# Units 1 and 3 to 11: state products and scores issued as one block, in other PSUM banks, with a step's second product moved behind them

## The chip, the cores and the metric

The kernel runs on one core of one Trainium2 chip. Its time is device microseconds from one launch; the figure compared is the median of the runs. TensorE does the matrix products (PE in the profile, PEld for its weight loads), VectorE (DVE), ScalarE (ACT) and GpSimd (POOL) do elementwise work, and SyncE (SP) issues most transfers.

## The reference

Two blocks follow each other. The first is a gated linear attention over 4 batches, 8 heads, 768 tokens and head size 48; the second is a feed-forward layer with ELU from 384 to 2048 and back to 384, on the 3072 tokens of the first:

```python
f = 1.0 / (1.0 + np.exp(-f_logit))
for t in range(S):
    state = f[:, :, t, :, None] * state + np.einsum('bhd,bhe->bhde', k[:, :, t], v[:, :, t])
    y[:, :, t] = np.einsum('bhd,bhde->bhe', q[:, :, t], state)
x = y.transpose(0, 2, 1, 3).reshape(B * S, H * D)
h = x @ w_in
g = np.where(h > 0.0, h, np.exp(np.minimum(h, 0.0)) - 1.0)
out = g @ w_out
```

The two weights arrive in 64-bit floating point and are narrowed on the chip.

## The kernel before

The tokens are cut into 12 units of 256 (three per batch). A unit's attention works in four chunks of 64 tokens; its feed-forward works in 8 positions P, each for 256 of the 2048 inner features.

The whole program is laid out by hand on a time line of steps T, 16 to a unit, two to a position. At an even T the list `plan[T]` runs and then `up(P)` issues the first product of position P; at an odd T `joined(P)` runs first (VectorE's three additions that finish the first product, then ScalarE's exponential), then `plan[T]`, then `down(P - 2)` issues the second product of the position two back. From unit 1 on both products are in a Strassen-like form with seven part products; `up7` writes two PSUM banks of tag `h` (`pa` and `pb`), and the next `up7` writes the same two, so it waits for the first addition `h[:, 0:2]` (for `pa`) and for `joined` (for `pb`). `elu` inside `up7` finishes the activation of the position before and lets GpSimd form `sums` for `down`. `down` accumulates a unit in banks `m0` to `m3`; at the last position ScalarE copies one half bank and VectorE's five additions at L991 read all four banks, before the store.

While unit u-1 runs its feed-forward, `attention(u)` is placed on the same steps. With t = 16(u-1), before the change: transposes of k at t+2 (banks `a0`, `a1`, copied by ScalarE), `advance` at t+4 (the chunks' products of k and v, L728, 64 records of 64x64 products into `a0`, `a1`), `step` for the four chunks at t+5 (VectorE adds each to the running state, L686, L691), `scores` at t+7 (products of q and k, L705, 64 records, also in `a0` and `a1`) followed by `mask` (two VectorE products with the causal mask, L713), `outputs` at t+9 (L743) and `carried` at t+11 (L763). Gates of the next unit (`decays`: a scan and a reciprocal on VectorE) stand at t+9, t+11, t+13. The range check of the weights rereads them in 32 pieces: `reread(n)` issues a transfer on SP at step 48+4n and `check(n)` reduces it on VectorE (two instructions, L603) four steps later.

Unit 0 to the first steps of unit 1 are the start: weights are fetched, narrowed on VectorE and ScalarE (L563, L567, L573, L581) and used in the same steps, with a feed-forward of unit 0 in plain form (L927 and L959, banks `m1` and `m2`) while unit 1's attention runs. `warm` issues matrix products that are used by nothing.

Of the kernel before, what the change touches and what calls it, by code (L numbers as in the profile page):

```python
# [356 lines left out]
def fast(ctx: ExitStack, tc: tile.TileContext, q, k, v, f_logit, w_in, w_out, out, flag, outer):  # L357
# [18 lines left out]
    nc = tc.nc  # L376
# [7 lines left out]
    NC = U // C  # L384
    UPB = S // U
    NU = B * UPB
    HP = H // 2
    NFT = DFF // 128
# [5 lines left out]
    LAG = 2  # L394
    AHEAD = 7
    WA = 1
    F1 = (1, 3)
    W0 = 3
    HOLD = 2
    A1 = (2, 5, 6, 8, 10, 11)  # L400
    D2 = (16, 18, 20, 22)
    A2 = (23, 25, 25, 26, 27, 28)
    D3 = (-7, -5, -3, -1)
    A3 = (2, 4, 5, 7, 9, 11)
    BL = 13
    RR = 0
    MX = 10
    CB = 16
    BL1 = 13
# [51 lines left out]
    start = ctx.enter_context(ExitStack())  # L461
# [215 lines left out]
    def step(u, c):  # L677

        if u % UPB == UPB - 1 and c == NC - 1:
            return  # L680
        new = pus[u][c % 2][:, c // 2]
        box = boxes[(u * NC + c) % len(boxes)]
        s = box[:].rearrange("n (p d) -> n p d", d=64)[:, 0:HP, PAD:]
        if u % UPB or c:
            old = sts[u, c][:].rearrange("n (p d) -> n p d", d=64)[:, 0:HP, PAD:]
            nc.vector.tensor_tensor(out=s, in0=new, in1=old, op=ALU.add)  # L686
        else:
            nc.scalar.copy(s, new)
        if c == NC - 1:
            end = qkf[u % NB]["f"][:, :, 1, U - 1 :].broadcast_to([128, HP, D])  # L690
            nc.vector.tensor_tensor(out=s, in0=s, in1=end, op=ALU.mult)  # L691
        sts[(u, c + 1) if c < NC - 1 else (u + 1, 0)] = box
# [25 lines left out]
    def advance(u, pairs=range(HP)):  # L718

        if u not in pus:  # L720
            pus[u] = [ps.tile([128, NW, HP, D], FP32, tag=n, name=f"psU{u}_{n}") for n in ("a0", "a1")]
        pu = pus[u]
        for p in pairs:
            for w in range(NW):
                for r in range(2):
                    h = 2 * p + r
                    for b in range(2):
                        nc.tensor.matmul(  # L728
                            pu[b][FULL[r], w, p], lhsT=kns[u, p // 2][FULL[b], p % 2, w, FULL[r]],
                            rhs=vs[u % NB][FULL[b], w, PAD + h * D : PAD + (h + 1) * D],  # L730
                            start=(w == 0 and p == 0), stop=(w == NW - 1 and p == HP - 1), skip_group_check=True,
                        )
# [91 lines left out]
    def at_step(step, *todo):  # L824
        plan.setdefault(step, []).extend(todo)

    def attention(u, first, then):

        kept = []
        for p, i in enumerate(first):  # L830
            at_step(i, (lambda: settle(u)) if p == NKT else lambda p=p: decays(u, p))
        if u > 1:
            at_step(then[0], lambda: transposed(u, 0, "a0"), lambda: transposed(u, 1, "a1"))
        at_step(then[1], lambda: advance(u))
        at_step(then[2], *(lambda c=c: step(u, c) for c in range(NC)))
        at_step(then[3], lambda: kept.append(scores(u)), lambda: mask(u, kept[0]))
        at_step(then[4], lambda: outputs(u))
        at_step(then[5], lambda: carried(u))

    gs, ss, pms, phs = {}, {}, {}, {}  # L840

# [108 lines left out]
    def down(P):  # L950
        m, j = order[P]
        if j == 0:
            pms[m] = [ps.tile([128, DM], FP32, tag=f"m{i + (m < DIRECT)}", name=f"psM{m}_{i}") for i in range(NW if m < DIRECT else 4)]
        pm, g = pms[m], gs.pop(P)
        ends = dict(start=(j == 0), stop=(j == NP - 1))
        if m < DIRECT:
            for i in range(2):
                for t in range(NW):
                    nc.tensor.matmul(  # L959
                        pm[t][:], lhsT=g[:, i, t * 128 : (t + 1) * 128], rhs=wo[:, 2 * j + i, :],  # L960
                        start=(j == 0 and i == 0), stop=(j == NP - 1 and i == 1),
                    )
            if j == NP - 1:
                o = (outer if (NU - m) % 2 else sb).tile([128, 2, DM], FP32, tag="o", name=f"o{m}", bufs=1)
                for t in range(NW):
                    nc.scalar.copy(o[:, t], pm[t][:])
                    t0 = m * U + t * 128
                    nc.sync.dma_start(out=out[t0 : t0 + 128, :], in_=o[:, t])
                del pms[m]
            return  # L970
        s = ss.pop(P)
        a = [[g[:, i, t * 128 : (t + 1) * 128] for i in range(2)] for t in range(2)]
        b = [[wo[:, 2 * j + i, h * DH : (h + 1) * DH] for h in range(2)] for i in range(2)]
        c = [combos[i][:, j] for i in range(4)]

        for bank, half, x, y in (
            (0, 0, a[0][0], b[0][0]), (3, 0, a[0][1], b[1][0]), (0, 1, s[:, 1], c[1]),
            (1, 0, s[:, 0], c[0]), (1, 1, s[:, 2], c[2]), (2, 1, a[1][1], c[3]), (2, 0, s[:, 3], b[1][1]),
        ):
            first = j == 0 and (bank, half) in ((0, 0), (3, 0), (1, 0), (2, 1))  # L980
            nc.tensor.matmul(  # L981
                pm[bank][:, half * DH : (half + 1) * DH], lhsT=x, rhs=y,
                start=first, stop=(j == NP - 1), skip_group_check=True,
            )
        if j == NP - 1:
            p = [[pm[i][:, h * DH : (h + 1) * DH] for h in range(2)] for i in range(4)]
            o = (outer if (NU - m) % 2 else sb).tile([128, 2, DM], FP32, tag="o", name=f"o{m}", bufs=1)
            u2 = sb.tile([128, DH], FP32, tag="u2", name=f"u2_{m}", bufs=1)
            u43 = sb.tile([128, 2, DH], FP32, tag="u43", name=f"u43_{m}", bufs=1)
            flat = o[:].rearrange("p t f -> p (t f)")  # L990
            add = lambda to, x, y: nc.vector.tensor_tensor(out=to, in0=x, in1=y, op=ALU.add)  # L991
            (nc.vector.tensor_copy if m == NU - 1 else nc.scalar.copy)(u2[:], p[0][0])
            add(flat[:, 0:DH], p[3][0], u2[:])
            add(u2[:], p[0][1], u2[:])
            add(u43[:], pm[1][:].rearrange("p (h f) -> p h f", h=2), u2[:].unsqueeze(1).broadcast_to([128, 2, DH]))
            add(flat[:, 3 * DH :], p[1][0], u43[:, 1])
            add(flat[:, DH : 3 * DH], pm[2][:], u43[:].rearrange("p h f -> p (h f)"))
            def store(*queues):
                for t in range(2):
                    for h in ((1, 0) if t else (0, 1)):  # L1000
                        queues[t].dma_start(
                            out=out[m * U + t * 128 : m * U + (t + 1) * 128, h * DH : (h + 1) * DH],
                            in_=o[:, t, h * DH : (h + 1) * DH],
                        )

            if m == NU - 1:
                left.append(store)
            else:
                store(nc.sync, nc.sync)
            del pms[m]  # L1010
# [18 lines left out]
        nc.tensor.matmul(pf[0:1, :], lhsT=low[:], rhs=causal[:, W - 1 : W], start=True, stop=True)  # L1029
        nc.vector.tensor_copy(flag[:], pf[0:1, :])  # L1030

    def warm(n, bank="m0"):

        pw = ps.tile([128, 4, 128], FP32, tag=bank, name="psW")
        for _ in range(n):
            nc.tensor.matmul(
                pw[:], lhsT=ident[:], rhs=ident[:].unsqueeze(1).broadcast_to([128, 4, 128]), start=True, stop=True
            )
# [81 lines left out]
    at_step(F1[1], lambda: move(1, 1, nc.scalar), lambda: watch(1))  # L1120
    at_step(F1[1] + 2, lambda: scale(1, ("q", NKT, nc.gpsimd)))
    at_step(A1[0], lambda: transposed(1, 0, "a0"), lambda: transposed(1, 1, "a1"))
    attention(1, (), A1)
    at_step(8, lambda: load(2))
    at_step(14, lambda: gates(2))
# [8 lines left out]
    for u in range(3, NU):  # L1134
        t = (u - 1) * NFT
        at_step(t + BL, lambda u=u: blend(u))
        at_step(t - 16, lambda u=u: load(u))
        at_step(t - 8, lambda u=u: gates(u))
        attention(u, [t + i for i in D3], [t + i for i in A3])
    for n in range(NR):  # L1140
        t = 3 * NFT + (NU - 4) * NFT * n // NR + RR
        at_step(t, lambda n=n: reread(n))
        at_step(t + 4, lambda n=n: check(n))
    at_step((NU - 1) * NFT + 9, lambda: finish_flag(0))
    at_step((NU - 1) * NFT + 13, lambda: finish_flag(1))
    for T in range(NU * NFT):
        P = T // 2
        sevens = order[P][0] >= DIRECT
        if T % 2 and sevens:
            joined(P)  # L1150
        if T % 2 == 0 and P and order[P - 1][0] < DIRECT:
            elu(P - 1)
        for f in plan.pop(T, ()):
            f()
        if T % 2 == 0:
            up(P)
        elif P >= LAG:
            down(P - LAG)
        for n in later.pop(T, ()):
            split(n)  # L1160
            lower(n)
# [53 lines left out]
```

## Time and profile before

| | |
|---|---|
| median of 3 runs | 567.14 us (567.03 to 568.18) |
| the profiled execution, first to last instruction | 567.3 us |
| TensorE busy, and its weight loads | 547.5 us (97%), 509.7 us (90%) |
| VectorE, ScalarE, GpSimd busy | 409.4 us (72%), 230.2 us (41%), 292.7 us (52%) |
| first products of the feed-forward in the final chain (L882) | 36% |
| second products in the final chain (L981) | 36% |
| scores, outputs, carried, state products in the final chain | 2% each |
| mean granted TensorE clock | 0.997 |

The page gives the profiled execution's span and no second time for it; the span lies 0.16 us over the median of the runs. The profile's line numbers are those of the kernel listing. An f32 product is recorded as two instructions, so a `down` of seven products is 14 records and an `up7` of ten is 20. In a timeline the first column is the start in us, the second the length of the merged group; groups of a pipelined engine overlap, so the distance from start to start is what a group costs.

### The profile page before, as it was taken

What the parts mean: (1) busy time and instruction counts of PE and PEld (TensorE: products, weight loads), DVE (VectorE), ACT (ScalarE), POOL (GpSimd) and SP (SyncE); (2) the same over time, 40 slices, a digit from 0 to 9 for tenths busy, and PEclk for the clock granted to TensorE, in tenths of its full rate; (3) what the DMA queues carried; (4) which work ended last, traced back from release to release, by engine and by line L of the source; (5) the groups of instructions that cost most, each with busy time, mean ns of one, the idle gap of its engine ahead of it and who ended that gap; (6) DMA issues with size and microseconds to landing.
All of it is one profiled execution on the core that took longest, in us unless ns stands there. A gap on an engine that the chain in (4) does not pass through costs nothing.

```text
span 567.3 us, 15527 instructions
## 1 busy us (share of the span) xinstructions
PE 547.5 (97%) x6336; PEld 509.7 (90%) x6336; DVE 409.4 (72%) x802; ACT 230.2 (41%) x424; POOL 292.7 (52%) x567
## 2 busy tenths in 40 slices
PE   6879998999999999999999999999999999999996
PEld 3566677999999999999999999999999999999996
DVE  8779989785675785885785885786776876745543
ACT  3287862443343433434343343333343343233331
POOL 6601788475374465456366357257248348325332
PEclk9899999999999999999999999999999999999999
DMA  8997951024024225215216216206206203201001
GB/s 212 266 261 209 298 129 43 3 47 114 3 46 138 65 52 145 79 42 156 78 36 155 86 38 153 86 19 173 84 14 178 84 6 74 84 2 36 29 2 35
DMA packets 38193, 53.30 MB, mean 94 GB/s; under 512 B 3712, under 2 KB 27936, under 8 KB 38112
## 3 DMA queue, kind: packets, MB, share of 16 engines
q1 hardware_dynamic: 37312, 51.62, 34.2%
q8 instruction: 52, 0.85, 0.7%
q10 hardware_dynamic: 800, 0.59, 0.4%
q14 instruction: 29, 0.24, 0.1%
HBM read 44.04 MB, written 4.72 MB: 86 GB/s over the span
## 4 chain that ended last, share of the span: by engine, by line
PE 81%; DMA 7%; DVE 7%; issue 2%; POOL 1%; ACT 1%; SPq 0%; DVEq 0%; ACTq 0%; POOLq 0%
PE psH L882 36%; PE psM L981 36%; DMA area<-in_moe_w_in_dram 4%; PE psS L705 2%; PE psY L743 2%; PE psY L763 2%; PE psU_a L728 2%; DVE f L631 2%; PE psT L669 1%; DMA xt<-xt 1%; DMA f<-f 1%; DVE f L626 1%; DMA k<-in_k_dram 1%; DVE bits L563 1%; DVE area L850 1%
## 5 line engine op out<-in xcount | busy, mean ns | idle before, releaser
L882 PE MATMUL psH<-xt,wi 128*128 128x128 f32 (+1 forms) x1056 | 195.0, 294 | 0.1
L946 POOL TENSOR_TENSOR sums<-gg 128x128 f32<-128x128 f32 x176 | 77.7, 462 | 214.5 <-DVE gg L936 205.9
L882 PEld LDWEIGHTS psH<-xt,wi 128*128 128x128 f32 x1056 | 149.5, 192 | 1.8 <-DVE hh L891 0.4
L914 ACT ACTIVATE gg<-hh 128x512 f32<-128x512 f32 x88 | 55.5, 631 | 232.0 <-DVE hh L904 154.6
L882 PE MATMUL psH<-xt,area 128*128 128x128 f32 x704 | 121.8, 275 | 1.3 <-DVE hh L904 1.0
L882 PEld LDWEIGHTS psH<-xt,area 128*128 128x128 f32 x704 | 106.5, 191 | 6.3 <-PE psH L882 1.3
L891 DVE TENSOR_TENSOR hh<-psH,u 128x256 f32<-128x256 f32 x88 | 37.1, 422 | 93.9 <-ACT u L889 93.9
L981 PE MATMUL psM<-area,sums 128*128 128x192 f32 x528 | 100.2, 326 | 0.0
L981 PEld LDWEIGHTS psM<-area,sums 128*128 128x128 f32 x528 | 88.2, 190 | 0.0
L981 PE MATMUL psM<-wo,gg 128*128 128x192 f32 x352 | 74.9, 335 | 0.0
L631 DVE RECIPROCAL f<-f 128x256 f32<-128x256 f32 x36 | 62.7, 1747 | 1.1
L936 DVE SCALAR_TENSOR_TENSOR gg<-gg,hh 128x512 f32<-128x512 f32 x88 | 61.9, 703 | 1.5 <-ACT gg L915 1.5
L915 ACT ACTIVATE gg<-gg 128x512 f32<-128x512 f32 x96 | 60.6, 631 | 3.0
L981 PEld LDWEIGHTS psM<-wo,gg 128*128 128x128 f32 x352 | 55.2, 190 | 2.0
L904 DVE TENSOR_TENSOR hh<-psH,u43h 128x256 f32<-128x256 f32 (+1 forms) x176 | 54.7, 352 | 3.0
L946 POOL TENSOR_TENSOR sums<-gg,sums 128x128 f32<-128x128 f32 x88 | 47.0, 534 | 6.9
L889 ACT COPY u<-psH 128x128 f32<-128x128 f32 x88 | 23.1, 263 | 60.9 <-PE psH L882 60.9
L621 POOL TENSOR_TENSOR q<-q,f 128x256 f32<-128x256 f32 x48 | 35.7, 745 | 21.8 <-DVE f L631 10.6
L904 DVE TENSOR_TENSOR u43h<-psH,hh 128x256 f32<-128x256 f32 x88 | 37.1, 422 | 12.7 <-PE psH L882 12.4
L621 POOL TENSOR_TENSOR k<-k,f 128x256 f32<-128x256 f32 x48 | 40.7, 851 | 7.1 <-DMA f<-f 5.1
L981 PE MATMUL psM<-area,gg 128*128 128x192 f32 x176 | 43.0, 326 | 0.0
L981 PE MATMUL psM<-wo,sums 128*128 128x192 f32 x176 | 43.0, 326 | 0.0
(97 smaller groups left out, 672.3 us busy)
## 6 DMA issues: line engine op xcount, KB each, us to landing
area<-in_moe_w_out_dram SPq DMA_DIRECT2D x8, 768.0 KB, 9.6
again<-in_moe_w_in_dram SPq DMA_DIRECT2D x16, 384.0 KB, 4.2
again<-in_moe_w_out_dram SPq DMA_DIRECT2D x16, 384.0 KB, 3.5
k<-in_k_dram SPq DMA_DIRECT2D x12, 384.0 KB, 4.5
q<-in_q_dram SPq DMA_DIRECT2D x12, 384.0 KB, 5.4
v<-in_v_dram SPq DMA_DIRECT2D x12, 384.0 KB, 5.8
area<-in_moe_w_in_dram SPq DMA_DIRECT2D x8, 576.0 KB, 8.4
out_dram<-o SPq DMA_DIRECT2D x42, 96.0 KB, 1.7
```

Of the source, the lines that this page charges most:

```text
L621: e.tensor_tensor(out=t[n][:, p], in0=t[n][:, p], in1=t["f"][:, p, "kq".index(n)], op=ALU.mult)
L631: nc.vector.reciprocal(f[:, p, 1], f[:, p, 0])
L705: nc.tensor.matmul(pc[r][FULL[b], w, p], lhsT=t["k"][FULL[r], p, cols], rhs=t["q"][FULL[r], p, cols], start=True, stop=True,)
L882: nc.tensor.matmul(to, lhsT=lhs, rhs=rhs, start=(n == 0), stop=True, skip_group_check=True)
L889: nc.scalar.copy(u1[:], pa[:, 0])
L891: add = lambda to, x, y: nc.vector.tensor_tensor(out=to, in0=x, in1=y, op=ALU.add)
L904: add = lambda to, x, y: nc.vector.tensor_tensor(out=to, in0=x, in1=y, op=ALU.add)
L914: nc.scalar.activation(g[:], h, AF.Relu, scale=-1.0)
L915: nc.scalar.activation(g[:], g[:], AF.Exp, scale=-1.0)
L936: nc.vector.scalar_tensor_tensor(out=g[:], in0=g[:], scalar=-1.0, in1=phs.pop(P), op0=ALU.add, op1=ALU.max)
L946: nc.gpsimd.tensor_tensor(out=s[:, i], in0=x, in1=y, op=op)
L981: nc.tensor.matmul(pm[bank][:, half * DH : (half + 1) * DH], lhsT=x, rhs=y, start=first, stop=(j == NP - 1), skip_group_check=True,)
```

## The change

For the ten units 1 and 3 to 11 the list of steps has four entries in place of six. A new function `both` issues at one step `advance`, `scores` into banks `m3` and `m0`, the two masks, and then the four state sums. For units 3 to 11 it stands at t+5, where before the state sums stood; for unit 1 at step 8, where its scores stood. So that `m3` and `m0` are free, the second product of the unit before at that step (its first, j = 0) is left out there and issued two steps later, directly ahead of the next one; its seven products are in another order (the ones for banks 1 and 2 first) at j = 0 of every unit from 1 on. Unit 2 keeps its six steps. All rereads and checks move by two steps (`RR`). At step 4 sixteen products of one element each are added on TensorE, ahead of that step's `up`.

```diff
+    SMALL = 16
+    RR = 2
-    A1 = (2, 5, 6, 8, 10, 11)
+    A1 = (2, 8, 10, 11)
-    A3 = (2, 4, 5, 7, 9, 11)
+    A3 = (2, 5, 9, 11)
-    RR = 0
...
+    def both(u):
+
+        advance(u)
+        mask(u, scores(u, ("m3", "m0")))
+        for c in range(NC):
+            step(u, c)
+
...
-        at_step(then[1], lambda: advance(u))
-        at_step(then[2], *(lambda c=c: step(u, c) for c in range(NC)))
-        at_step(then[3], lambda: kept.append(scores(u)), lambda: mask(u, kept[0]))
-        at_step(then[4], lambda: outputs(u))
-        at_step(then[5], lambda: carried(u))
+        if len(then) == 4:
+            at_step(then[1], lambda: both(u))
+        else:
+            at_step(then[1], lambda: advance(u))
+            at_step(then[2], *(lambda c=c: step(u, c) for c in range(NC)))
+            at_step(then[3], lambda: kept.append(scores(u)), lambda: mask(u, kept[0]))
+        at_step(then[-2], lambda: outputs(u))
+        at_step(then[-1], lambda: carried(u))
...
-        for bank, half, x, y in (
+        todo = [
             (0, 0, a[0][0], b[0][0]), (3, 0, a[0][1], b[1][0]), (0, 1, s[:, 1], c[1]),
             (1, 0, s[:, 0], c[0]), (1, 1, s[:, 2], c[2]), (2, 1, a[1][1], c[3]), (2, 0, s[:, 3], b[1][1]),
-        ):
+        ]
+        if j == 0:
+            todo = todo[3:] + todo[:3]
+        for bank, half, x, y in todo:
...
-    def warm(n, bank="m0"):
+    def warm(n, bank="m0", small=0):
...
+        for _ in range(small):
+            nc.tensor.matmul(pw[0:1, 0, 0:1], lhsT=ident[:, 0:1], rhs=ident[:, 0:1], start=True, stop=True)
...
+    at_step(4, lambda: warm(0, "m3", SMALL))
...
+    joint = [(u - 1) * NFT + A3[1] for u in range(3, NU)]
...
-        elif P >= LAG:
+        elif P >= LAG and T not in joint:
+            if T - 2 in joint:
+                down(P - LAG - 1)
             down(P - LAG)
```

## The prediction

> **What bounds the kernel now.** I read the page's busy shares and chain first, then all waits from 104 us to the end, then TensorE's timeline over one unit, then VectorE's over the same steps.
>
> ```profile
> PE 547.5 (97%) x6336; PEld 509.7 (90%) x6336; DVE 409.4 (72%) x802; ACT 230.2 (41%) x424; POOL 292.7 (52%) x567
> ...
> PEclk9899999999999999999999999999999999999999
> ...
> PE 81%; DMA 7%; DVE 7%; issue 2%; POOL 1%; ACT 1%; SPq 0%; DVEq 0%; ACTq 0%; POOLq 0%
> ```
>
> TensorE is the bound, at full clock; the chain's DMA and DVE shares lie in the first 100 us. Of the waits after 104 us, TensorE's largest is this (total, times, longest):
>
> ```profile
> PEld psU_a L728 <- issue: 2.0, 9, 0.2
> ```
>
> Nothing else on TensorE waits there for more than 0.2 us in all. So in this part only work taken off TensorE itself can shorten the span. The nine waits stand ahead of the nine state blocks, and the timeline shows what they are:
>
> ```profile
> 310.92 1.15 PE L728 MATMUL psU_a<-v,kn 64*64 64x48 f32 x64
> 312.00 0.49 PE L882 MATMUL psH<-xt,wi 128*128 128x128 f32 x2
> 312.33 0.39 PE L882 MATMUL psH<-xt,area 128*128 128x128 f32 x2
> ...
> 319.04 0.39 PE L882 MATMUL psH<-xt,wi 128*128 128x128 f32 x2
> 319.36 1.16 PE L705 MATMUL psS<-q,k 64*64 64x64 f32 x64
> 320.45 0.92 PE L981 MATMUL psM<-wo,gg 128*128 128x192 f32 x4
> 321.20 1.14 PE L981 MATMUL psM<-area,sums 128*128 128x192 f32 x6
> ...
> 337.05 0.39 PE L882 MATMUL psH<-xt,wi 128*128 128x128 f32 x2
> 337.27 0.82 PE L981 MATMUL psM<-wo,gg 128*128 128x192 f32 x4
> 337.92 1.14 PE L981 MATMUL psM<-area,sums 128*128 128x192 f32 x6
> ```
>
> Without a block two L882 records take 0.22 us (337.05 to 337.27) and four L981 records 0.65. With scores between, the same take 0.32 and 0.75: 0.10 us is lost going into a block of 64x64 products and 0.10 coming out. The state block likewise (0.33 for the two records behind it). A block itself is 1.08 to 1.09 us. The check: an up and a down are 2.44 + 2.28 = 4.72; from one L981 to the next with a block it is 6.00 (320.45 to 326.45), so 1.28 = 1.09 + 0.19. A unit is 8 x 4.72 + 0.87 (transposes) + 4 x 1.28 = 43.75, and the measured stretches are 43.83, 43.75 and 43.74. Nothing is left over.
>
> **What the skill says.** The Trainium skill, "TensorEngine Tiling (Array Packing)", Key Properties, states that changing the tiling mode drains TensorE, changing the tile within a mode not. The trace agrees with both: 0.19 to 0.20 us per block as above, and none where the start has state products and scores next to each other:
>
> ```profile
> 16.65 0.45 PE L728 MATMUL psU_a<-v,kn 64*64 64x48 f32 x16
> 16.96 0.46 PE L705 MATMUL psS<-q,k 64*64 64x64 f32 x16
> 17.24 0.40 PE L728 MATMUL psU_a<-v,kn 64*64 64x48 f32 x16
> ```
>
> 0.31 and 0.28 us for 16 records, 17 to 19 ns each, against 17 in a block of 64. The page "TensorE: Matmul & The Clock Gate", Architectural detail, says VectorE and ScalarE are strict FIFO; the timeline shows them in program order, so each moved VectorE instruction delays all behind it.
>
> **The change, part by part.**
>
> *One block in place of two, units 3 to 11.* Removed: one way in and one way out, 0.19 to 0.20 us a unit; 9 x 0.195 = 1.75 us. The 128 records stay. Postponing down (j = 0) adds none: down follows down, the same shape.
>
> *Does TensorE wait anywhere new?* I lay the new order on the unit at 310.82, where down of step t+3 ends. Up (t+4) runs to 313.26; the way in 0.10; state products to 314.44; scores to 315.53; up (t+6) starts, with 0.11 of way out, and its first `pb` product comes 1.00 later, at 316.53; it ends at 318.08, both downs at 322.64, where the old order has 322.83. VectorE's rows there:
>
> ```profile
> 312.97 0.82 DVE L991 TENSOR_TENSOR o<-psM,u 128x192 f32<-128x192 f32 x2
> 313.71 1.00 DVE L603 TENSOR_REDUCE spans<-again 128x1 f32<-128x384 f32 x2
> 314.63 0.41 DVE L891 TENSOR_TENSOR hh<-psH,u 128x256 f32<-128x256 f32 x1
> ...
> 316.01 0.62 DVE L904 TENSOR_TENSOR hh<-psH,u43h 128x256 f32<-128x256 f32 x2
> 316.55 1.52 DVE L686 TENSOR_TENSOR state<-psU_a,state 128x192 f32<-128x192 f32 x4
> ```
>
> - Banks `m3`, `m0`: last read by the additions at 311.46 and 311.92, done by 312.3; scores need them at 314.44. Slack 2.1.
> - `pa` and `pb` of t+4: the old rows from 314.63 to 316.63 move up by the check (0.92, 313.71 to 314.63), which leaves this step: `h` is done at 314.1, `joined` at 315.7. Needed at 315.53 and 316.53: slack 1.4 and 0.8. This 0.8 is the tightest; with the check still there `joined` would end at 316.63, 0.1 late. That is what the shift of the checks is worth.
> - Then VectorE: masks from 315.65 (1.20), state sums (1.84 to 318.39 in the old rows), the check now at t+6 (0.92): 319.6. `h` 320.0, ELU 320.6, `joined` 321.6. The next up wants `pa` at 322.64 and `pb` at 323.5: slack 2.6 and 1.9.
> - Postponed down: masks end at 316.9; with banks 1 and 2 first it touches 0 and 3 after four products (4 x 0.33) at 319.4. Slack 2.5.
> - Queued behind the waiting mask are the state sums, needed by carried at t+11, over 10 us later; behind those the check and `h`, counted above. Outputs (t+9) want the masks 8 us later.
>
> The other moved checks fall at t+2, t+10, t+14. At t+2 VectorE sat idle 3.26 us, at t+10 1.22, each over 0.92; at t+14 `joined` ends near 344.0 against a need at 345.2. The rereads move on SP with the checks, four steps apart as before (3.4 to 5.2 us to land, over 9 us of room); none now stands behind the stores. Cost nothing; uncovered, 0.92 each.
>
> *Unit 1.* In the start VectorE is busy without a gap from 37 to 61 us. Two waits matter: 2.30 us ahead of up at 38.69 (for VectorE's narrowing), and 1.24 us before scores (50.76 to 52.00), which need `a0`, `a1` back from the state sums. In banks `m3`, `m0` that wait goes, but moving the state block out of step 5 exposes another: down would end at 44.2, and the next up needs weights ready at 45.2. So up runs 45.25 to 48.0, down to 50.76, the merged block 50.86 to 53.03; up began at 53.08. VectorE has the same rows to do by 58. I take 0, bounds -0.6 (the 0.57 wait before carried at 63.37) and +0.6 (VectorE's split slipping).
>
> *Sixteen one-element products.* No row shows them in series. The one at L1029 has two records; the skill's Tiling page, Instruction Overhead, gives about 60 cycles each, at 2.4 GHz 25 ns: an estimate of 16 x 2 x 25 = 0.8 us. They stand in the 2.30 us wait: 0. Uncovered, 0.8; a gain is possible where they hold the clock up (0.50 at 25 to 27 us, after 1.35 us of idling), but it reads 1.00 from 36 to 40: none taken.
>
> *Order of the first second-product in unit 1.* It now wants `sums` first; GpSimd has them at 90.4 to 91.75, the product starts at 91.40 and needs the last at 92.4: 0.
>
> Sum: -1.75 + 0 + 0 = -1.75, against the span of 567.3. The median is 0.16 lower: 567.14 - 1.75 = 565.4; rounded 565.4.
>
> **Rivals.** *B, no gain:* the way between state products and scores costs as much as a way out and in, or another small wait eats 0.2 us a unit: 566.2 to 568.2. For it: only short neighbouring blocks show otherwise, at the start. *C, slower:* the 0.8 us at `pb` isn't there, because VectorE's run after the additions is later than its old rows say. From 0.8 + 0.2 us of lateness a unit it decides; at 1.4 TensorE waits 0.6 a unit, 9 x (0.6 - 0.2) = +3.6: 570.7. For it: five additions, three of `up`, two waits on ScalarE lie in one strict queue. Against: these rows repeat within 0.1 us from unit to unit. *D, more:* unit 1's waits go without others taking their place, -1.2 more (the wait for `a0`, `a1`): 564.2. Against: VectorE has no gap there.
>
> **Chances.** A measurement tells a change from none at about 0.2%, 1.13 us. Likeliest 0.67 (564.7 to 566.0), D 0.07, B 0.15, C 0.11. Faster: 0.67 + 0.07 less 0.02 for spread at the edge = 0.72; same 0.16; slower 0.12. Eight in ten: from 564.1, half of D, to 567.0, part of B.
>
> **What would show it.** Per unit one stretch of 128 records at L729 and L706 of about 2.17 us with one wait ahead; units of 43.55 us; no TensorE wait for DVE at `psH` in steps t+6 and t+8; between 40 and 63 us, a wait of about 1 us before the fourth up where none was, and none before scores. A gap between L729 and L706 would mean B, a wait for `hh` at `psH` C. The clock falling in the 2.2 us of small products would make all of it wrong.

## The result

| | before | after |
|---|---|---|
| median of 10 runs each | 568.46 us (567.03 to 570.23) | 565.93 us (565.16 to 567.29) |
| the profiled execution, first to last instruction | 567.3 us | 563.5 us |
| TensorE busy | 547.5 us | 544.1 us |
| a unit, mean of eight (transposes of unit 3 to those of unit 11) | 43.76 us | 43.41 us |

The ratio of after to before is 0.9963, with a 95% interval of 0.9946 to 0.9979: 2.1 us less, at least 1.2 and at most 3.1. A second set of 14 runs gave 0.9964 (0.9949 to 0.9978). The median of before is 1.3 us above the one shown ahead of the change, which came from the first three of these ten runs. One later run of before, beside some of the experiments, took 935.58 us at a granted clock of 0.559 and is left out of their ratios.

The page of after, the same lines as were shown of before:

```profile
PE 544.1 (97%) x6368; PEld 508.7 (90%) x6368; DVE 407.1 (72%) x802; ACT 228.7 (41%) x424; POOL 293.5 (52%) x567
...
PEclk9999999999999999999999999999999999999999
...
PE 84%; DVE 8%; ACT 3%; issue 3%; POOL 1%; DMA 1%; ACTq 0%; DVEq 0%; POOLq 0%
```

TensorE is still the bound. It has 32 records more (the one-element products) and 3.4 us less of busy time. Everything that TensorE's matmuls and weight loads waited for from 104 us to the end (total, times, longest):

```profile
PEld psS L706 <- PE psM L995: 0.2, 1, 0.2
PEld psY L764 <- ACT between L751: 0.2, 1, 0.2
PEld psM L995 <- issue: 0.2, 1, 0.2
```

The nine waits ahead of the state blocks are gone, and none for VectorE came in their place. The last line is new and is taken up below. TensorE's timeline around one merged block:

```profile
310.31 0.39 PE L893 MATMUL psH<-xt,wi 128*128 128x128 f32 x2
310.62 1.15 PE L729 MATMUL psU_a<-v,kn 64*64 64x48 f32 x64
311.59 1.14 PE L706 MATMUL psS<-q,k 64*64 64x64 f32 x64
312.66 0.49 PE L893 MATMUL psH<-xt,wi 128*128 128x128 f32 x2
312.99 0.39 PE L893 MATMUL psH<-xt,area 128*128 128x128 f32 x2
313.21 0.61 PE L893 MATMUL psH<-xt,wi 128*128 128x128 f32 x4
313.65 0.61 PE L893 MATMUL psH<-xt,area 128*128 128x128 f32 x4
```

From start to start: 0.31 for two records ahead of the block (0.22 without one), 0.97 for the state products, 1.07 for the scores, 0.33 for the two records behind. The block took 2.04 us, not 2.17. The state products alone took 1.08 in before, and 0.97 where scores follow them: 0.11 lies at the end of a block, before the next full-array product starts, and the start-to-start distance had put it into the block. It is called the emptying below. The weight loads show the edges too:

```profile
310.62 1.02 PEld L729 LDWEIGHTS psU_a<-v,kn 64*64 64x64 f32 x64
311.55 1.04 PEld L706 LDWEIGHTS psS<-q,k 64*64 64x64 f32 x64
312.66 0.30 PEld L893 LDWEIGHTS psH<-xt,wi 128*128 128x128 f32 x2
312.88 0.30 PEld L893 LDWEIGHTS psH<-xt,area 128*128 128x128 f32 x2
```

At both edges of the block the first weight load starts together with its own product (310.62 and 312.66). Between the two halves it runs 0.04 ahead (311.55 for the product at 311.59), and among full-array products 0.11 ahead (312.88 for the one at 312.99). Whether the array has to be empty at an edge, or only the weight load can't run ahead there, these runs don't tell apart. VectorE's rows beside the block:

```profile
310.24 0.82 DVE L1005 TENSOR_TENSOR o<-psM,u 128x192 f32<-128x192 f32 x2
310.98 0.41 DVE L902 TENSOR_TENSOR hh<-psH,u 128x256 f32<-128x256 f32 x1
...
312.36 0.62 DVE L915 TENSOR_TENSOR hh<-psH,u43h 128x256 f32<-128x256 f32 x2
312.90 1.28 DVE L714 TENSOR_TENSOR at<-psS,twice 128x512 f32<-128x512 f32 x2
314.09 1.52 DVE L687 TENSOR_TENSOR state<-psU_a,state 128x192 f32<-128x192 f32 x4
315.65 0.36 DVE L692 TENSOR_TENSOR state<-state,f 128x192 f32<-128x192 f32 x1
315.93 1.00 DVE L604 TENSOR_REDUCE spans<-again 128x1 f32<-128x384 f32 x2
```

`joined` ends at 312.98 and `pb` is first needed at 313.65 (the last row of TensorE's timeline above): 0.67 us to spare by the rows. The check stands behind masks and state sums, two steps later than it was.

**The 3.8 us between the two profiled executions, by stretches** (differences of the starts in the two timelines):

| stretch | before | after | difference |
|---|---|---|---|
| to the first `up` | 30.06 | 28.64 | -1.42 |
| from there to the first `up7` (unit 1) | 47.61 | 47.99 | +0.38 |
| to the transposes of unit 3 | 52.52 | 52.25 | -0.27 |
| to the transposes of unit 11 (eight merged blocks) | 350.11 | 347.25 | -2.86 |
| to VectorE's last pair of additions (the ninth) | 82.36 | 82.32 | -0.04 |
| from there to the end (stores) | 4.64 | 5.05 | +0.41 |

The first row is not the change. Up to there the two programs hold the same instructions; the execution profiled of before had TensorE at half clock just ahead of it. Its window of 26 to 28 us (length, busy time and records of each engine in the order PE, PEld, DVE, ACT, POOL, then the granted clock, DMA share, GB/s):

```profile
26.00:28.00 2.00, 2.00 (x54) 1.88 (x56) 0.00 (x0) 0.00 (x0) 0.00 (x0) 0.51 1.00 342
```

and that of after:

```profile
26.00:28.00 2.00, 1.09 (x54) 0.86 (x44) 1.01 (x2) 0.85 (x2) 0.12 (x1) 1.00 1.01 299
```

The kernel before with its checks alone moved (below) started its first `up` at 28.92 with the same code up to there. The clock is not the whole of it: a second execution of the changed kernel started its first `up` at 27.55, 1.1 us before the one above, both at full clock up to there. So two profiled executions of the same code may differ by over a microsecond here, and only stretches past it are compared from here on.

### The profile page after: what moved, and what is told of

The parts are those of the page before. It is cut to its first block, busy times and chain, and to the rows that moved or that the text cites. A ratio compares the mean times of both kernels' runs of the same rounds, so it can differ in the third digit from the quotient of the medians.

```text
span 563.5 us, 15590 instructions
## 1 busy us (share of the span) xinstructions
PE 544.1 (97%) x6368; PEld 508.7 (90%) x6368; DVE 407.1 (72%) x802; ACT 228.7 (41%) x424; POOL 293.5 (52%) x567
## 4 chain that ended last, share of the span: by engine, by line
PE 84%; DVE 8%; ACT 3%; issue 3%; POOL 1%; DMA 1%; ACTq 0%; DVEq 0%; POOLq 0%
PE psH L893 37%; PE psM L995 36%; PE psU_a L729 2%; PE psS L706 2%; PE psY L744 2%; PE psY L764 2%; PE psT L670 2%; DVE f L632 2%; ACT area L574 1%; PE psW L1052 1%; DVE bits L564 1%; DMA f<-f 1%; DVE area L568 1%; PE psY L809 1%; DVE wi L582 1%
## 5 line engine op out<-in xcount | busy, mean ns | idle before, releaser
L995 PE MATMUL psM<-area,sums 128*128 128x192 f32 x528 | 102.2, 326 | 0.0
L947 DVE SCALAR_TENSOR_TENSOR gg<-gg,hh 128x512 f32<-128x512 f32 x88 | 64.1, 728 | 1.5 <-ACT gg L926 1.5
L622 POOL TENSOR_TENSOR q<-q,f 128x256 f32<-128x256 f32 x48 | 38.9, 812 | 21.7 <-DVE f L632 8.7
L957 POOL TENSOR_TENSOR sums<-sums,gg 128x128 f32<-128x128 f32 x88 | 43.9, 498 | 0.0
```

What stands on the lines that cost most here:

```text
L622: e.tensor_tensor(out=t[n][:, p], in0=t[n][:, p], in1=t["f"][:, p, "kq".index(n)], op=ALU.mult)
L947: nc.vector.scalar_tensor_tensor(out=g[:], in0=g[:], scalar=-1.0, in1=phs.pop(P), op0=ALU.add, op1=ALU.max)
L957: nc.gpsimd.tensor_tensor(out=s[:, i], in0=x, in1=y, op=op)
L995: nc.tensor.matmul(pm[bank][:, half * DH : (half + 1) * DH], lhsT=x, rhs=y, start=first, stop=(j == NP - 1), skip_group_check=True,)
```

## The experiments

The theory of the prediction: the gain is the price of a way into and out of a block of 64x64 products, paid once less in each of nine units, and moving the checks is what keeps VectorE from taking it back. The rivals: the gain comes from something else (the checks, unit 1), or the price goes by the number of products and not by the block.

**A full-array product between the two halves**, and the same product ahead of the block as its control:

```diff
         advance(u)
+        if u > 1:
+            one = ps.tile([128, 512], FP32, tag="m1", name=f"psX{u}")
+            nc.tensor.matmul(one[:, 0:1], lhsT=ident[:], rhs=ident[:, 0:1], start=True, stop=True)
         mask(u, scores(u, ("m3", "m0")))
```

> The changed kernel with one full-array product of one column between state products and scores of units 3 to 11, so that the joined block is cut in two again. Theory M (a block of 64x64 products costs a change of mode in and out, 0.35 us with the emptying inside the block): state products and scores of a unit take about 2.45 us in place of 2.04, a unit 43.80 in place of 43.40, the whole 3.5 us more than the changed kernel. Theory Q (the gain comes from VectorE's new order and waits that went): only the product itself, 0.05 us a unit, 0.5 us in all.

> The control: the same one-column product, but ahead of the state products, where the array is in full mode anyway. Theory M: 0.05 us a unit, units of 43.45, 0.5 us in all. If the product itself costs what it costs between the two, units of 43.80 here too, and the run before it proves nothing on the mode.

Measured: ratio to before 1.0037 (1.0024 to 1.0050) with the product between, 1.0038 (1.0023 to 1.0053) with it ahead; a unit took 43.86 and 43.88 us, against 43.41. (Without one unit of 44.44, in which TensorE once stood still for 0.5 us, the second is 43.80.) The control cost nearly as much as the test, so the times decide nothing: a lone one-column product costs some 0.3 us wherever it stands, against the 0.05 that was expected of the control, and the control has a wait of 0.2 ahead of it as well. TensorE's timeline with the product between tells more:

```profile
312.18 1.15 PE L729 MATMUL psU_a<-v,kn 64*64 64x48 f32 x64
313.26 0.38 PE L833 MATMUL psX<-ident 128*128 128x1 f32 x2
313.57 1.16 PE L706 MATMUL psS<-q,k 64*64 64x64 f32 x64
```

and with it ahead:

```profile
312.18 0.35 PE L832 MATMUL psX<-ident 128*128 128x1 f32 x2
312.47 1.15 PE L729 MATMUL psU_a<-v,kn 64*64 64x48 f32 x64
313.44 1.13 PE L706 MATMUL psS<-q,k 64*64 64x64 f32 x64
```

The same 64 state products take 1.08 us where a product of the full array follows and 0.97 where scores follow. The product itself takes 0.31 and 0.29. So 0.11 of a block's price sits at its end, inside the block's own row.

**Two blocks again, all else as changed**, and then only a quarter of the state products apart:

```diff
     def both(u):
-        advance(u)
+        if u == 1:
+            advance(u)
...
         if len(then) == 4:
+            if u > 1:
+                at_step(then[1] - 1, lambda: advance(u))
             at_step(then[1], lambda: both(u))
```

In the second, the line in `attention` issues `advance(u, (0,))`, one of the four pairs of heads, and `both` issues `advance(u, (1, 2, 3))`.

> The changed kernel with the state products of units 3 to 11 back at their old step, one up ahead of the scores, and nothing else altered: the same instructions, banks, postponed product, masks and checks, but two blocks of 64 records in place of one of 128. Theory M (a change of mode in and out costs 0.35 us a block, emptying included): units of 43.76 as before the change, +3.2 us on the changed kernel. Theory Q (the gain comes from VectorE's order, the banks or the checks): units of 43.41, no difference.

> As the one before, but only the first head pair's 16 records go to the old step, 112 stay in the joined block. Theory M, with the price per block: units of 43.76 again, +3.2 us on the changed kernel. If the loss goes by records: an eighth to a quarter of it, 43.45 to 43.50.

Measured: two blocks 1.0017 (1.0003 to 1.0031), a unit 43.74 us; a quarter apart 1.0005 (0.9992 to 1.0018), a unit 43.75. Against the changed kernel that is 0.33 and 0.34 us a unit. The price doesn't go by the number of products: 16 records apart cost what 64 do. TensorE's timeline with the quarter apart, and its waits:

```profile
309.22 0.49 PE L997 MATMUL psM<-wo,sums 128*128 128x192 f32 x2
309.64 0.45 PE L729 MATMUL psU_a<-v,kn 64*64 64x48 f32 x16
310.02 0.49 PE L895 MATMUL psH<-xt,wi 128*128 128x128 f32 x2
310.34 0.39 PE L895 MATMUL psH<-xt,area 128*128 128x128 f32 x2
```

```profile
PEld psU_a L729 <- issue: 2.0, 9, 0.2
```

Two L997 records take 0.42 here and 0.32 elsewhere: 0.10 in. The 16 products take 0.38, where a quarter of 0.97 is 0.24: 0.14 at its end. The next two records take 0.32 for 0.22: 0.10 out. Sum 0.34, as the unit's length says. The wait line of the kernel before is back, nine times 0.2. It adds nothing to this sum: in before the scores, which had no such wait, cost the same 0.10 going in.

**The checks at their old steps**, and, the other way round, the kernel before with its checks two steps later:

```diff
-    RR = 2
+    RR = 0
```

> The changed kernel with the rereads and checks back at their old steps. The slack at pb was put at 0.8 us and is 0.67 in the trace of the changed kernel, a check is 0.92. Theory: TensorE waits about 0.3 us at psH for hh in each of nine units, units of 43.7, 2.5 us more than the changed kernel. Rival (the move of the checks does nothing): units of 43.40, 0.

> The kernel before with the rereads and checks two steps on and nothing else. Theory: TensorE waits for VectorE nowhere in units 3 to 11 there, so units stay at 43.76 and the time within 0.2% of before. Rival (the checks give the gain): 1 to 3 us less.

Measured: checks back 1.0026 (1.0011 to 1.0040), a unit 43.81; before with later checks 1.0005 (0.9989 to 1.0022), a unit 43.74. Alone they bring nothing; with the checks at their old steps the merged block loses 0.40 a unit, more than it gains. (Unit 3 has no check yet, and its unit took 43.40; in the other seven the loss is 0.46.) TensorE behind the merged block, checks back:

```profile
316.28 0.49 PE L893 MATMUL psH<-xt,wi 128*128 128x128 f32 x2
...
316.83 0.61 PE L893 MATMUL psH<-xt,wi 128*128 128x128 f32 x4
317.66 0.68 PE L893 MATMUL psH<-xt,area 128*128 128x128 f32 x4 [0.23 <-DVE hh L915]
```

and VectorE ahead of it:

```profile
314.60 1.00 DVE L604 TENSOR_REDUCE spans<-again 128x1 f32<-128x384 f32 x2
315.52 0.41 DVE L902 TENSOR_TENSOR hh<-psH,u 128x256 f32<-128x256 f32 x1
...
316.90 0.62 DVE L915 TENSOR_TENSOR hh<-psH,u43h 128x256 f32<-128x256 f32 x2
```

From 316.83 to 317.66 is 0.83 for four records that take 0.44 in the changed kernel: 0.39 lost, at the first product of `pb`, on VectorE's third addition, which ends at 317.52. The four records of `pb` then take 0.52 us, to 318.18, for 0.45 in the changed kernel, which makes the 0.46.

**Unit 1 in its old six steps**, without the one-element products; and only these products left out:

```diff
-    A1 = (2, 8, 10, 11)
+    A1 = (2, 5, 6, 8, 10, 11)
...
-    at_step(4, lambda: warm(0, "m3", SMALL))
```

> The changed kernel with unit 1 at its six old steps and without the sixteen one-element products; units 3 to 11 joined as before. Theory (unit 1 gives nothing): the wait before scores returns (about 1.2 us), the one before up (1.26 us) goes, the wait before carried falls from 1.63 to 0.6, and the unit's feed-forward starts 0 to 0.6 us earlier: -0.4 us, between -1.0 and +0.6. Rival (unit 1 gives part of the gain): +1.2 us or more.

> The changed kernel without the sixteen one-element products at step 4, unit 1 still joined. If their time (0.94 us in the trace) lies inside a wait for VectorE, as predicted, the stretch from the first up to unit 1's first product stays at 47.9 us; if they stand on the path, it falls by up to 0.9 us, to 47.0, and unit 1's loss was theirs and not that of the joined block.

Measured: six steps 0.9949 (0.9929 to 0.9970); the products left out, one run, 565.02 us. The stretch from the first `up` to the first `up7`:

| kernel | unit 1 | us |
|---|---|---|
| before | six steps | 47.61 |
| before, checks later | six steps | 47.47 |
| changed, unit 1 in six steps | six steps | 47.37 |
| changed | one block | 47.99 |
| changed, second set | one block | 47.86 |
| changed, without one-element products | one block | 47.86 |

The one-element products cost nothing here: 0.94 us for 32 records, inside the wait for the narrowed weights, which read 2.30 without them. Unit 1's block costs 0.4 to 0.6: over all kernels profiled here the stretch is 47.84 to 48.07 in nine executions with the block and 47.37 to 47.61 in four with six steps. TensorE in the changed kernel, with the idle time ahead of a group in brackets:

```profile
35.12 0.94 PE L1050 MATMUL psW<-ident 128*1 128x1 f32 x32
37.26 2.83 PE L938 MATMUL psH<-xt,wi 128*128 128x256 f32 x12 [1.20 <-DVE wi L582]
...
43.93 2.83 PE L938 MATMUL psH<-xt,wi 128*128 128x256 f32 x12 [1.26 <-DVE wi L582]
...
49.27 1.15 PE L729 MATMUL psU_a<-v,kn 64*64 64x48 f32 x64
50.24 1.13 PE L706 MATMUL psS<-q,k 64*64 64x64 f32 x64
...
62.33 1.35 PE L764 MATMUL psY<-q,state 64*64 64x64 f32 x64 [1.63 <-ACT between L751]
```

The wait ahead of scores (1.24) is gone, the one ahead of the fourth `up` (1.26) is new, as forecast. What was not forecast is the last: carried waits 1.63 us for ScalarE's copies `between`, where in before it was 0.57. Over all executions it is 1.38 to 1.79 with the joined block and 0.37 to 1.06 with six steps. ScalarE's rows there:

```profile
58.11 1.95 ACT L574 ACTIVATE area<-area 128x768 uint16<-128x768 uint32 x1 [2.66 <-DVE area L568]
60.34 1.93 ACT L574 ACTIVATE area<-area 128x768 uint16<-128x768 uint32 x1 [0.27 <-DVE area L568]
62.01 0.47 ACT L751 COPY between<-psY 128x8 f32<-128x8 f32 x2
```

The copies are queued behind two pieces of narrowing, and the first of these had waited 2.66 us for VectorE, which from 53.7 to 56.9 did masks and state sums in one go. That these two rows are the cause is read from the trace; no run moved them alone.

**The second products in their old bank order:**

```diff
-        if j == 0:
-            todo = todo[3:] + todo[:3]
```

> The changed kernel with the old order of the seven products at j = 0, banks 0 and 3 first. Theory: the masks end 1.2 us before these banks are wanted even so, no wait in units 3 to 11, and the 0.27 us that the changed kernel loses at the first second-product of the last unit (bank 1 first, which VectorE reads last) goes: -0.3 us. Rival: the downs wait for the masks, 0.3 us or more in each of nine units, +2.7 us.

Measured: 0.9954 (0.9935 to 0.9972), a unit 43.43. The loss is at one place, the last unit, whose first `down` is not put off. The changed kernel:

```profile
526.48 0.39 PE L893 MATMUL psH<-xt,wi 128*128 128x128 f32 x2
526.91 0.89 PE L995 MATMUL psM<-area,sums 128*128 128x192 f32 x4
```

and the old order:

```profile
526.41 0.39 PE L893 MATMUL psH<-xt,wi 128*128 128x128 f32 x2
526.63 0.82 PE L993 MATMUL psM<-wo,gg 128*128 128x192 f32 x4
```

0.43 and 0.22 for the same two records, and the four behind take 0.73 for 0.65. From unit 11's transposes to VectorE's last additions the kernels with the new order take 82.32 us (four executions, the changed kernel's included), those with the old one 82.03 and 82.04 (two executions). With the new order the first product writes bank 1, which VectorE's additions for the unit before read among the last; this is the wait of 0.2 at `psM` that was new in the waits of after, and it isn't in those of the old order.

**All three together:** the changed kernel without unit 1's block, without the one-element products and with the old bank order, beside the changed kernel once more.

> The changed kernel without what the runs so far say brings nothing: unit 1 back to its six steps and without the sixteen one-element products (as in e4), and the second products in their old bank order (as in e5). If those two differences add, it lies 0.6 + 0.3 = 0.9 us below the changed kernel beside it (ratio to before about 0.9945 if that one is at 0.996), with a period of 43.41 us a unit and 47.4 us from the first up to unit 1's first product. If unit 1's loss in the traces was only a different start of each execution, it lies 0.3 below, within what the runs can tell.

> The changed kernel as it is, once more, on the chip of e10: ratio 0.996, period 43.41 us, 47.9 us from the first up to unit 1's first product, in this second execution as in the first if the length of that stretch belongs to the kernel. If the start differs from one execution to the next by the clock, this shows in a clock below 0.9 before 28 us and in the first up's start, not in that stretch.

Measured: 564.89 us, 0.9952 (0.9936 to 0.9969), against 566.13 us, 0.9964 (0.9949 to 0.9978). In the traces the two savings add: 47.37 for 47.86 in the start, 82.04 for 82.32 at the end, units of 43.41 in both: 0.77 us. It is the best version by the traces. By the times its lead over the changed kernel is not told apart, since the intervals overlap; its lead over the kernel before is.

Outputs and carried in one block too, to save another way in and out, wasn't tried.

## Why the prediction was right, and where it was off

The direction and the mechanism held: 565.4 was predicted, 565.93 measured, in the range. That it came so near is in part luck: the block's gain was taken 1.3 us too small, two losses of 0.8 us together were put at nothing, and the median that it started from was 1.3 us low. The block is one, its nine waits are gone, TensorE waits nowhere new in units 3 to 11.

- **One block in place of two: the term was mis-sized.** Predicted 0.19 to 0.20 a unit, 1.75 us in nine; the unit's length fell by 0.36 (43.76 to 43.41, with two units of 43.83 in the execution of before that the others didn't have), and putting the block apart again cost 0.33 and 0.34. The step that failed is "A block itself is 1.08 to 1.09 us", taken as pure work because 64 records at 17 ns matched the start's 16 at 17 to 19. In a row 64 take 0.97; the other 0.11 is the emptying, paid once a block, and joins the 0.10 in and 0.10 out. Nine blocks are worth 3.0 to 3.2 us. What the Trainium skill says in "TensorEngine Tiling (Array Packing)", Key Properties, that a change of mode drains TensorE and a change of tile doesn't, fits these runs: 0.31 to 0.36 us a block, whether it holds 16 or 64 records.
- **Slack at `pb`:** predicted 0.8, measured 0.67; the missing 0.13 is the block's shorter end, after which `pb` is wanted sooner. VectorE ran as its old rows say, the additions included. With the check left in place 0.1 of lateness was predicted; the shift was worth 0.40 a unit. The lateness by the rows is 0.92 - 0.67 = 0.25, and TensorE resumed 0.14 after VectorE's last row ended, which the prediction had left out of the slack. So the wait that rival C named is what the kernel without the shift shows, though not for C's reason: VectorE's rows are no later than the old ones. In the changed kernel it is 0.67 us away by the rows, 0.53 with the 0.14.
- **Other moved checks, rereads, one-element products: 0.** Held: later checks alone changed nothing, no wait for them appears, and the products' 0.94 us (estimate 0.8) lie in the wait that covers them.
- **Unit 1: 0, between -0.6 and +0.6.** It is +0.4 to +0.6. The forecast for the fourth `up` and for the scores was right; the split of VectorE's work did slip, and it came out at carried, over ScalarE. Rival D's extra gain did not come.
- **Order of the first second product:** it was worked out for unit 1, where it is 0, and not for unit 11, where the order also holds: +0.28.
- **Against the span:** the median was taken as 0.16 under the span. Each run of after lies 1.7 to 1.9 us over its own span (565.24 for the profiled 563.5). At that distance the profiled execution of before belongs to a time near 569.0, above all three of the runs shown with it. This fault had little effect on the forecast, since the difference was taken from the median shown. But that median was 1.3 low: from the median of ten the same -1.75 gives 566.7, and the change that the ratio gives is -2.1.

By the traces the sum is -3.0 (nine blocks at 0.33) + 0.5 (unit 1) + 0.28 (unit 11) = -2.2, and the times say -2.1, from -3.1 to -1.2. The 0.4 more at the stores' end in after's profile is not counted: from VectorE's last additions to the end it is 4.6 to 5.3 us over all these kernels, without order. The 0.27 less before unit 3 is not counted either: a second execution of the changed kernel has 52.51 there, and the other kernels with the block have 52.14 to 52.53.

## What to carry to other kernels

The price of changing TensorE's tiling is not all in the gaps around a block: compare a block followed by its own kind with one followed by another, and count 0.3 us or more a block (here 0.31 to 0.36), for 16 records as for 64. Moving work together also puts VectorE's share of it in one run, so look for the first consumer behind that run (here `pb`, with 0.67 us left) and move something optional out of it. At the start, where VectorE and ScalarE are full, the same merge cost time: apply such a change only where the engines beside it have room.

## What the runs showed of the hardware

- A one-column f32 product of the full array took 0.29 to 0.31 us beside 64x64 blocks, about as long as 20 of the small records; sixteen one-element products in a row took 0.94 us for 32 records, 29 ns each.
- The half clock comes in some executions and not in others of the same code. In before it stood ahead of the first `up`; the kernel with its checks alone moved, the same code up to there, had none. In three of the thirteen executions profiled it fell later, on an `up` behind a wait for narrowed weights: in the best version, in the kernel with the old bank order and in the one with the checks at their old steps. The first two:

```profile
36.77 4.51 PE L938 MATMUL psH<-xt,wi 128*128 128x256 f32 x12 [2.30 <-DVE wi L582]
```

```profile
37.26 4.51 PE L938 MATMUL psH<-xt,wi 128*128 128x256 f32 x12 [1.44 <-DVE wi L582]
```

That `up` takes 2.83 us at full clock, yet the stretch around it was no longer: 47.37 us in the best version, the same as in the kernel with unit 1 in six steps and no such fall, and 47.86 with the old bank order, the same as in the changed kernel's second execution, which had no fall. VectorE was busy for 9.8 of the 10 us from 34 to 44 us in both, which speaks for VectorE setting the pace there. The one-element products didn't keep the clock up: the last two of the three kernels have them just ahead of that `up`. It fell there in two of eight executions with them and in one of five without. The Trainium skill, "TensorE: Matmul & The Clock Gate", Part 1, calls the ramp at a kernel's start run-variable; these falls, later in the kernel, vary between executions of the same code as well.
